# Batch 0's attention as a written-out software pipeline, its denominators on DVE, and the sign of the float64 weights moved from ACT to DVE

## The chip, the cores and the metric

The kernel runs on one core of a Trainium2 chip. The metric is the device time of one execution in microseconds; of each kernel several executions are timed and the median is given. One execution of each kernel is also profiled, and all rows below are from that one. The engines are called PE (TensorE, matrix products), DVE (VectorE), ACT (ScalarE), POOL (GpSimd) and SP (SyncE, which here only starts transfers). PE's clock has two levels, 2.4 GHz (written as a granted clock of 1.00) and 1.2 GHz (0.50).

## The reference

Three blocks follow one another on 4 sequences of 576 positions: attention with 8 heads of 64, a feed-forward block 512 to 2048 to 512 with layer norm and residual, and a mixture of 8 experts, of which each position uses one.

```python
scores = scale * np.matmul(q, k.transpose(0, 1, 3, 2))
mask_local = (rel >= 0) & (rel < stride)          # heads 0 to 3, stride 32
mask_strided = (rel >= 0) & (pos[None, :] % stride == pos[:, None] % stride)   # heads 4 to 7
scores = np.where(masks[None, :, :, :], scores, -1000000000.0)
scores = scores - np.max(scores, axis=-1, keepdims=True)
attn = np.exp(scores)
attn = attn / (np.sum(attn, axis=-1, keepdims=True) + 1e-09)
x = np.matmul(attn, v)                            # heads side by side: 512 columns
xn = (x - mu) / np.sqrt(var + 1e-06) * g_ln
x = x + np.maximum(xn @ w_ch1, 0.0) @ w_ch2
# then: an expert e per position, out = p[e] * (relu(x @ w1[e]) @ w2[e])
```

The feed-forward weights `w_ch1` and `w_ch2` arrive as float64: random float32 numbers were multiplied by a float64 factor.

## The kernel before

**Attention.** Heads are taken in pairs (`pairs`; hp 0 and 1 are local, 2 and 3 strided), and each pair is cut into three units of 3 or 4 groups (`GROUPS`). Batch 0 has four pairs, so twelve units, in the order hp 0, 2, 3, 1. A unit goes through five steps: `st_scores` (products of q with k into one PSUM tile `ps_sc`, then a maximum per row), `st_exp` (EXP on ACT), `st_norm`, `st_trans` (transposes on PE into `ps_pt`, copied to SBUF as `pt` by ACT) and `st_out` (products with v into `ps_o`, from there into `xt`, the input of the next block). `prep` transposes q and k of a pair ahead of its units; it writes them to `qbd` and `kT`.

Two ways of doing this stand side by side. In batch 0 (`FAST`) the mask is added on PE, by a product of the identity with the mask in bf16 (L300) that opens the accumulation; DVE takes the maximum (L316) and subtracts it (L317), one EXP covers the unit (L328), the denominators come from products of a constant matrix with `pt` (L372), and DVE reads them (L378), takes their RECIPROCAL over all columns (L379) and multiplies the output by it (L397). In the other batches one custom DVE instruction per group (L320) adds the mask and gives the extremum, one EXP per group (L331) also gives the sum, and `st_norm` does an addition, a RECIPROCAL on 3 or 4 columns (L341) and a scaling (L342).

Batch 0 runs alone at the start, in the loop at the end of the setup. Per turn it calls up to five steps for different units, and the scheduler of the framework then places the instructions by its own estimates, unless `keep` pins an instruction to the program's order. `st_out` adds two products of 256 columns (`keep_clock`, L285) that write to a tile nobody reads. The loads are dealt out on SP's queue by `ORD`, small ones between large ones.

**The feed-forward block.** 2304 positions are cut into 9 chunks of 256; chunk c has 16 slices f of the hidden layer, and for each `mm1` (L613, 12 products), a ReLU split in two parts (ACT L615, DVE L616) and `mm2` (L629, 12 products). The list `order` starts with chunk 0 alone, then mixes chunks 0 and 1. `ln_0`, `ln_2` and `ln_split` make chunk 0's normalized input `xc` (mean products L510 and L516, copy L523, subtraction L525, scaling L596 and L597). Attention of batches 1 to 3 is laid into this block at the places `SPANS`.

**The weights.** 32 tiles of 128x512 float64 numbers are turned into float32 by integer work, and then into a high and a low part (fp32r): `w_low` shifts the low word on DVE (L443); `w_sign` on ACT writes the sign as a half float into the low word (L449) and takes the absolute value of the high word (L450); `w_high` joins the words on DVE (L455); `w_split` casts (L469, by DVE for the first four tiles, by ACT after that) and POOL subtracts (L470). `turns` and `joins` list what is done in which turn, and `weights_next` does one turn; six turns fall in the attention of batch 0, the others in the feed-forward block while chunks 0 and 1 are worked on.

## Time and profile before

| what | us |
|---|---|
| median of 3 runs (lowest to highest) | 916.74 (914.50 to 918.66) |
| the profiled execution, its time | 914.36 |
| its span, first to last instruction | 912.5 |
| PE busy | 873.2 (96%) |
| DVE busy | 474.3 (52%) |
| ACT busy | 368.9 (40%) |
| POOL busy | 152.2 (17%) |

Busy times are unions of the instructions' times on an engine; a matrix product's record contains its latency, so PE reads as busy also where products leave room. The mean granted clock of PE is 0.962 over the span. The shares are averages over stages that differ much: the first 72 us, in which batch 0's attention runs, have to be looked at by themselves. Where a row has a bracket at its end, it is the idle time of the engine ahead of the first of these instructions and what ended it.

### The profile page before, as it was taken

The numbers are of one execution on the slowest core, as the hardware profiler recorded it, in microseconds if no ns is written. First come the engines' busy times: TensorE is split into PE (matmuls) and PEld (weight loads), VectorE is DVE, ScalarE is ACT, GpSimd is POOL, SyncE is SP. The second block draws the span as 40 slices with busy tenths as digits, with TensorE's granted clock in tenths as the row PEclk, the third lists the DMA queues.
The fourth block names the chain that finished last, engine by engine and source line by source line (L and its number), as shares of the span: only waits on it lengthen the run. The fifth ranks groups of instructions, "written<-read, shape, count | busy, mean of one in ns | idle before, by whom it ended". The sixth has DMA issues, their size and how long they took to land. (4 is left out here: it accounts for less than half of the span.)

```text
span 912.5 us, 18019 instructions
## 1 busy us (share of the span) xinstructions
PE 873.2 (96%) x6644; PEld 782.2 (86%) x6644; DVE 474.3 (52%) x1560; ACT 368.9 (40%) x919; POOL 152.2 (17%) x163
## 2 busy tenths in 40 slices
PE   7888899899999999999999999999999999999994
PEld 5657888899999999899999999999877787787773
DVE  3778756537775646657555464675722134111541
ACT  2448879943354423354231212242112244222551
POOL 2013323312020020120121212020131111110100
PEclk8757989999999999999999999999999999999999
DMA  9850444310222201210000000511374364510730
GB/s 218 219 188 1 117 108 133 91 48 1 74 52 62 57 2 27 68 43 17 28 2 24 2 24 1 185 49 47 139 265 143 139 224 157 194 48 24 285 114 15
DMA packets 95024, 82.92 MB, mean 91 GB/s; under 512 B 67395, under 2 KB 75589, under 8 KB 94920
## 3 DMA queue, kind: packets, MB, share of 16 engines
q1 hardware_dynamic: 87656, 65.41, 24.2%
q0 software_dynamic: 3632, 11.11, 3.6%
q10 hardware_dynamic: 3632, 5.09, 1.6%
q8 instruction: 55, 0.90, 0.4%
q14 instruction: 49, 0.40, 0.1%
HBM read 72.08 MB, written 10.30 MB: 90 GB/s over the span
## 5 line engine op out<-in xcount | busy, mean ns | idle before, releaser
L629 PE MATMUL acc<-h,w 128*128 128x256 f32 x1728 | 246.2, 290 | 1.0 <-DVE h L616 1.0
L613 PE MATMUL ps_h<-xc,w 128*128 128x256 f32 x1728 | 242.6, 288 | 2.5 <-ACT xc L596 1.7
L613 PEld LDWEIGHTS ps_h<-xc,w 128*128 128x128 f32 x1728 | 222.7, 195 | 5.8 <-ACT xc L596 2.4
L629 PEld LDWEIGHTS acc<-h,w 128*128 128x128 f32 x1728 | 219.9, 192 | 3.6 <-DVE h L616 1.4
L615 ACT ACTIVATE h<-ps_h 128x256 fp32r<-128x256 f32 x144 | 55.6, 386 | 220.6 <-PE ps_h L613 206.1
L616 DVE SCALAR_TENSOR_TENSOR h<-ps_h,h 128x256 fp32r<-128x256 f32 x144 | 60.7, 421 | 93.7 <-ACT h L615 93.3
L1341 PE MATMUL ps_h<-wx,xs 128*128 128x512 f32 x360 | 87.6, 398 | 0.8 <-DVEq L1268 0.8
L1369 PE MATMUL ps_y<-wx,ht 128*128 128x512 f32 x360 | 85.9, 394 | 0.0
L1341 PEld LDWEIGHTS ps_h<-wx,xs 128*128 128x128 f32 x360 | 66.6, 188 | 15.8 <-DVEq L1268 1.3
L1369 PEld LDWEIGHTS ps_y<-wx,ht 128*128 128x128 f32 x360 | 66.5, 188 | 13.3
L470 POOL TENSOR_TENSOR w<-stg,w 128x512 fp32r<-128x512 f32 x32 | 45.2, 1412 | 136.1 <-ACT w L469 69.6
L1372 ACT ACTIVATE y<-ps_y,pr 128x512 f32<-128x512 f32 x19 | 13.1, 688 | 89.2 <-PE ps_y L1369 61.6
L331 ACT ACTIVATE sm<-sm,st 108x54 f32<-108x54 f32 (+1 forms) x120 | 41.4, 348 | 15.5 <-DVE st L320 15.3
L449 ACT ACTIVATE stg<-stg 128x512 f16<-128x512 f32 x32 | 43.9, 1371 | 0.7 <-DVE stg L443 0.6
L867 DVE TENSOR_TENSOR xs<-ps_tx,xs 128x512 fp32r<-128x512 f32 x15 | 10.4, 691 | 64.0 <-ACTq L1268 45.8
L1344 ACT ACTIVATE h<-ps_h 128x512 f32<-128x512 f32 x30 | 16.3, 595 | 62.0 <-PE ps_h L1341 62.0
L759 DVE TENSOR_TENSOR wx<-raw,wx 128x1024 fp32r<-128x1024 f32 x32 | 37.5, 1220 | 1.7 <-ACT wx L756 1.3
L304 PE MATMUL ps_sc<-kT,qbd 128*128 128x96 f32 (+1 forms) x280 | 34.8, 263 | 1.6 <-DVE xt L399 0.7
L304 PEld LDWEIGHTS ps_sc<-kT,qbd 128*128 128x128 f32 (+1 forms) x280 | 32.2, 182 | 2.9 <-DVE xt L399 0.9
L756 ACT CAST wx<-raw 128x1024 fp32r<-128x1024 f32 x32 | 31.8, 1061 | 5.7 <-PE acc L629 4.1
L1373 POOL DMA_INDIRECT out_dram<-y,idx x15 | 15.1, 1005 | 113.0 <-ACT y L1372 71.3
L455 DVE SCALAR_TENSOR_TENSOR stg<-stg 128x512 int32<-128x512 int32 x32 | 25.1, 785 | 15.3 <-ACT stg L450 14.9
(375 smaller groups left out, 1203.9 us busy)
## 6 DMA issues: line engine op xcount, KB each, us to landing
stg<-in_moe_w_ch_dram SPq DMA_DIRECT2D x32, 512.0 KB
raw<-in_moe_w_dram SPq DMA_DIRECT2D x16, 1024.0 KB
raws<-in_moe_w_dram SPq DMA_DIRECT2D x16, 1024.0 KB
...
```

The lines of the kernel that those rows point to most:

```text
L304: pe.matmul(ps[0:m, i, :], qbd[:, q0:q0 + w, :].rearrange("p s j -> p (s j)"), kT[:, k0:k0 + n], start=not fast, stop=not fast or i == ng - 1)
L331: act.activation(sm[0:m, i, :], sm[0:m, i, :], AF.Exp, bias=st[0:m, 0, i:i + 1], scale=-1.0, accum_out=st[0:m, 1, i:i + 1])
L449: keep(act.activation(t.bitcast(F16)[..., 1], f32(t[..., 1]), AF.Copy, scale=2.0 ** -112))
L470: keep(pool.tensor_tensor(w[:, 1], r, f32(w[:, 0]), op=ALU.subtract))
L613: pe.matmul(ps, w[:, a, d, o:o + 128], xcs[c][:, b_, d, :], start=(i == 0), stop=(i == 11))
L615: act.activation(h[:, 0, :], ps, AF.Relu)
L616: dve.scalar_tensor_tensor(h[:, 1, :], ps, 0.0, f32(h[:, 0, :]), op0=ALU.max, op1=ALU.subtract)
L629: pe.matmul(accs[c][d // 2][:, d % 2, :], w[:, a, f % 2, d * 128:(d + 1) * 128], h[:, b_, :], start=(f == 0 and (a, b_) == (0, 0) and d % ...
L756: act.copy(wx[i][:, 0, :], raw[i // 2][:, i % 2, :])
L759: dve.tensor_tensor(wx[i][:, 1, :], raw[i // 2][:, i % 2, :], f32(wx[i][:, 0, :]), op=ALU.subtract)
L1341: pe.matmul(hp_[fg], s_[:, a, d, :], wx[d][:, b_, 512 * fg:512 * fg + 512], start=(i == 0), stop=(i == 11))
L1369: pe.matmul(ps, s_[a][:, f, :], wx[4 + f // 2][:, b_, 512 * (f % 2):512 * (f % 2) + 512], start=(i == 0), stop=(i == 23))
```

## The change

- `MODES` takes the place of `FAST` and gives each unit one of three ways. Mode 2 (batch 0, hp 0 and 2): mask by PE, DVE takes only the minimum, and ACT reads the scores from PSUM, one EXP per group with the minimum as bias. Mode 1 (batch 0, hp 3 and 1, and all of batch 1): mask by PE, minimum and subtraction on DVE, one EXP per unit. Mode 0 (batches 2 and 3) is the way that batches 1 to 3 had. So batch 1 changes from mode 0 to mode 1.
- In modes 1 and 2 DVE sums the EXPs over the keys, and `st_norm` then does what it did in mode 0. The denominator products, the wide RECIPROCAL and the final multiplication are gone; `st_out` copies, on DVE in mode 2 and on ACT in mode 1 of batch 0.
- q is scaled by -1/8 where `prep` copies it, so the scores come out negated and the maximum becomes a minimum.
- Batch 0's loop is written out: step i does the scores of unit i, the normalization of unit i-1, the transposes of i-2 and the output of i-3, and all instructions of PE, ACT and DVE in it are kept in the program's order (`Pin`). At the end of each step stand five products of 512 columns on zeros (six in the first three steps), and two after each of the first pair's two `prep` calls.
- `prep` of batch 0 takes its PSUM tiles from another pool (`ps_m`), and a fourth buffer for the EXPs is added (`SM0`).
- Loads of batch 0 come pair by pair, the first weight tile after three pairs.
- The sign of a weight: `w_low` gets a second DVE instruction that masks the sign bit of the high word and joins it to the low word; ACT's L449 goes.

```diff
...
-FAST = (0,)
+MODES = {(0, 0): 2, (0, 2): 2, (0, 3): 1, (0, 1): 1, 1: 1}
...
-NEG = -1.0e9 / SCALE
+NEG = -1.0e9
...
-SMB, SM0, PT0, TL = 2, 3, 2, 1
-WARM0, WARM, LB = 10, 2, 5
+SMB, SM0, PT0, TL = 2, 4, 2, 1
+WARM0, WARM, LB = 10, 5, 5
...
-    pe, act, dve, pool, sp = nc.tensor, nc.scalar, nc.vector, nc.gpsimd, nc.sync
+    pinned = [False]
+    class Pin:
+        def __init__(self, eng):
+            self.eng = eng
+        def __getattr__(self, name):
+            fn = getattr(self.eng, name)
+            if not pinned[0] or name == "dma_start":
+                return fn
+            return lambda *args, **kw: tc.keep_in_program_order(fn(*args, **kw))
+    pe, act, dve = Pin(nc.tensor), Pin(nc.scalar), Pin(nc.vector)
+    pool, sp = nc.gpsimd, nc.sync
...
-            ps = side_r([128, 3 * QT], "ps_tr")
+            ps = (ps_m.tile([128, 512], F32, tag="m", name="ps_tr")[:, 0:3 * QT] if b == 0 else side_r([128, 3 * QT], "ps_tr"))
...
-                act.copy(dst(qbd[0:64, 0:S, 0]), s_[0:64])
-                (act.copy if half and b else dve.tensor_copy)(dst(qbd[64:128, 0:S, 1]), s_[64:128])
+                act.activation(dst(qbd[0:64, 0:S, 0]), s_[0:64], AF.Copy, scale=-SCALE)
+                if half and b:
+                    act.activation(dst(qbd[64:128, 0:S, 1]), s_[64:128], AF.Copy, scale=-SCALE)
+                else:
+                    dve.tensor_scalar(dst(qbd[64:128, 0:S, 1]), s_[64:128], -SCALE, None, op0=ALU.mult)
...
+    def mode_of(b, hp):
+        return MODES.get((b, hp), MODES.get(b, 0))
...
-        fast = b in FAST
+        mode = mode_of(b, hp)
...
-        if fast:
+        if mode:
...
-            pe.matmul(ps[0:m, i, :], qbd[:, q0:q0 + w, :].rearrange("p s j -> p (s j)"), kT[:, k0:k0 + n], start=not fast, stop=not fast or i == ng - 1)
+            pe.matmul(ps[0:m, i, :], qbd[:, q0:q0 + w, :].rearrange("p s j -> p (s j)"), kT[:, k0:k0 + n], start=not mode, stop=not mode or i == ng - 1)
...
-        sms[b, hp, u0] = (sm, st)
-        if fast:
-            mx = st[0:m, 0, 0:ng]
-            return [lambda: dve.tensor_reduce(mx, ps[0:m], axis=AX.X, op=ALU.max),
-                    lambda: dve.tensor_tensor(sm[0:m], ps[0:m], mx.unsqueeze(2).to_broadcast([m, ng, n]), op=ALU.subtract)]
+        sms[b, hp, u0] = (sm, st, ps)
+        mn = st[0:m, 0, 0:ng]
+        if mode:
+            new = [lambda: dve.tensor_reduce(mn, ps[0:m], axis=AX.X, op=ALU.min)]
+            if mode == 1:
+                new.append(lambda: dve.tensor_tensor(sm[0:m], ps[0:m], mn.unsqueeze(2).to_broadcast([m, ng, n]), op=ALU.subtract))
+            return new
         def part(i):
-            dve.tensor_tensor_reduce(sm[0:m, i, :], ps[0:m, i, :], mask(i), -SCALE, 3.0e38, ALU.add, ALU.min, st[0:m, 0, i:i + 1])
+            dve.tensor_tensor_reduce(sm[0:m, i, :], ps[0:m, i, :], mask(i), 1.0, 3.0e38, ALU.add, ALU.min, st[0:m, 0, i:i + 1])
...
     def st_exp(b, hp, u0):
...
-        if b in FAST:
-            act.activation(sm[0:m], sm[0:m], AF.Exp, scale=SCALE)
+        mode = mode_of(b, hp)
+        if mode == 1:
+            act.activation(sm[0:m], sm[0:m], AF.Exp, scale=-1.0)
...
-            act.activation(sm[0:m, i, :], sm[0:m, i, :], AF.Exp, bias=st[0:m, 0, i:i + 1], scale=-1.0, accum_out=st[0:m, 1, i:i + 1])
+            act.activation(sm[0:m, i, :], (ps if mode else sm)[0:m, i, :], AF.Exp, bias=st[0:m, 0, i:i + 1], scale=-1.0, **({} if mode else dict(accum_out=st[0:m, 1, i:i + 1])))
     def st_norm(b, hp, u0):
...
-        if b in FAST:
-            return []
-        return [
+        todo = [
             lambda: dve.tensor_scalar(rs, rs, 1e-9, None, op0=ALU.add),
...
+        if mode_of(b, hp):
+            todo.insert(0, lambda: dve.tensor_reduce(rs, sm[0:m], axis=AX.X, op=ALU.add))
+        return todo
     def st_trans(b, hp, u0):
...
-        fast = b in FAST
-        ps = side([128, 2, ng, w] if fast else [128, 1, ng, w], "ps_o")
+        ps = side([128, ng, w], "ps_o")
...
-                pe.matmul(ps[64 * j:64 * j + 64, 0, i, 0:k], vv[0:min(n, k) if hp > 1 else n, i, j, :], pt[0:min(n, k) if hp > 1 else n, i, j:2 * k:2], start=True, stop=True)
-        if fast:
-            for j in range(2):
-                pe.matmul(ps[64 * j:64 * j + 64, 1], mean_w[0:n, 0:64], pt[0:n, :, j::2], start=True, stop=True)
-        if b == 0:
-            keep_clock(pt.rearrange("p g m -> p (g m)")[0:n, 0:256].bitcast(BF16).rearrange("p (n w) -> p n w", w=2)[:, :, 1], WARM)
-        o = ps[:, 0].rearrange("p g q -> p (g q)")
-        if fast:
-            rs = pt.rearrange("p g m -> p (g m)")[:, 0:ng * w]
-            dve.tensor_scalar(rs, ps[:, 1].rearrange("p g q -> p (g q)"), float(DM), 1e-9, op0=ALU.mult, op1=ALU.add)
-            dve.reciprocal(rs, rs)
+                pe.matmul(ps[64 * j:64 * j + 64, i, 0:k], vv[0:min(n, k) if hp > 1 else n, i, j, :], pt[0:min(n, k) if hp > 1 else n, i, j:2 * k:2], start=True, stop=True)
+        o = ps.rearrange("p g q -> p (g q)")
...
-            if fast:
-                dve.tensor_tensor(dst, cut(o), cut(rs), op=ALU.mult)
-            else:
-                (dve.tensor_copy if i % 2 else act.copy)(dst, cut(o))
+            (dve.tensor_copy if (i % 2 if b else mode_of(b, hp) > 1) else act.copy)(dst, cut(o))
...
         keep(dve.tensor_single_scalar(t[..., 0], t[..., 0], 29, op=ALU.logical_shift_right))
+        keep(dve.scalar_tensor_tensor(t[..., 0], t[..., 1], -2 ** 31, t[..., 0], op0=ALU.bitwise_and, op1=ALU.bitwise_or))
...
-        keep(act.activation(t.bitcast(F16)[..., 1], f32(t[..., 1]), AF.Copy, scale=2.0 ** -112))
         keep(act.activation(f32(t[..., 1]), f32(t[..., 1]), AF.Abs, scale=2.0 ** -112))
...
-    def weights_next():
-        for fn, i in turns[nw[0]] + joins[nw[0]]:
+    def weights_turn():
+        for fn, i in turns[nw[0]]:
...
+    joined = [0]
+    def weights_join():
+        while joined[0] < nw[0]:
+            for fn, i in joins[joined[0]]:
+                fn(i)
+            joined[0] += 1
+    def weights_next():
+        weights_turn()
+        weights_join()
...
-    load_qk(*pairs[0])
-    load_v0(0)
-    load_qk(*pairs[1])
-    big = [hold(load_w, 0), hold(load_w, 1), hold(load_qk, *pairs[2]), hold(load_w, 2), hold(load_w, 3), hold(load_qk, *pairs[3]), hold(load_w, 4), hold(load_w, 5)]
-    small = [hold(load_v0, i) for i in range(1, 4)]
-    for n in ORD:
-        load_mixed(sum((big[i] for i in n[0]), []), sum((small[i] for i in n[1]), []))
+    for i in range(4):
+        load_qk(*pairs[i])
+        load_v0(i)
+        if i > 1:
+            load_w(i - 2)
+    for i in range(2, W_START):
+        load_w(i)
...
-    while pos[0] < NSTEP or any(fifo.values()):
-        i = pos[0]
-        do_x, do_n = bool(fifo["x"]), take("n", 1)
-        do_t, do_o = bool(fifo["t"]), bool(fifo["o"])
-        if do_x:
-            do("x")
-        if i < NSTEP:
-            begin(do_n)
-        else:
-            pos[0] += 1
-            for p in [p for un in do_n for p in st_norm(*un)]:
-                p()
-            fifo["t"] += do_n
-        if do_t:
-            do("t")
-        if do_o:
-            un = fifo["o"][0]
-            do("o")
-            if un == (0, 1, 0):
-                ln_0()
-            if un == (0, 1, 3):
-                ln0 = [ln_2, ln_split]
-        if i > WI and nw[0] < W_START * (i - WI) // (NSTEP + 2 - WI):
-            weights_next()
+    pinned[0] = True
+    us = [(b, hp, u0) for b, hp in pairs[:4] for u0, _ in GROUPS[hp]]
+    for nm in "qk":
+        prep(*pairs[0], nm)
+        keep_clock(idle, 2)
+    for i in range(len(us) + 3):
+        new, old = st_scores(*us[i]) if i < len(us) else [], st_norm(*us[i - 1]) if 0 < i <= len(us) else []
+        for p in old + new:
+            p()
+        if 1 < i < len(us) + 2:
+            st_trans(*us[i - 2])
+        if i > 2:
+            st_out(*us[i - 3])
+        if i < len(us):
+            st_exp(*us[i])
+        weights_join()
+        if i < 9 and i % 3:
+            prep(*pairs[i // 3 + 1], "qk"[i % 3 - 1])
+        keep_clock(idle, WARM + (i < 3))
+        if i > 2 and us[i - 3] == (0, 1, 0):
+            ln_0()
+        if i > 2 and us[i - 3] == (0, 1, 3):
+            ln0 = [ln_2, ln_split]
+        if i > WI and nw[0] < W_START:
+            weights_turn()
...
+    weights_join()
+    pinned[0] = False
...
```

How the order moves on the engines is shown at three places. All instructions of the written-out loop have one line in the new program, L84.

DVE in the front, where the scores of units 9 and 10 meet the output of unit 6. `st` holds extremum and sum, `first` the EXPs, `stg` a weight tile. Before:

```order
L316 TENSOR_REDUCE st<-ps_sc 128x3
L378 TENSOR_SCALAR first<-ps_o 128x216
L317 TENSOR_TENSOR first<-ps_sc,st 128x288
L379 RECIPROCAL first<-first 128x216
L316 TENSOR_REDUCE st<-ps_sc 128x3
L397 TENSOR_TENSOR xt_331<-ps_o,first 128x12x8
L397 TENSOR_TENSOR xt_362<-ps_o,first 128x12x8
L397 TENSOR_TENSOR xt_387<-ps_o,first 128x12x2
```

Now (step 10, from the normalization of unit 9 to the conversion of weights behind it):

```order
L84 TENSOR_REDUCE st<-first 128x3
L84 TENSOR_SCALAR st<-st 128x3
L84 RECIPROCAL st<-st 128x3
L84 TENSOR_TENSOR first<-first,st 128x288
L84 TENSOR_REDUCE st<-ps_sc 128x3
L84 TENSOR_TENSOR first<-ps_sc,st 128x288
L84 SCALAR_TENSOR_TENSOR stg<-stg 128x512
L84 CAST w_0_600<-stg 128x4x128
L84 TENSOR_SCALAR stg<-stg 128x512
L84 SCALAR_TENSOR_TENSOR stg<-stg 128x512
```

The sum and three operations on few columns take the place of the read and the RECIPROCAL on 216 columns, and each step ends with the weights' four instructions, of which the last is the sign.

PE at the end of the front, the last units' transposes (`ps_pt`) and outputs (`ps_o`). Before:

```order
L350 MATMUL ps_pt<-iw,first 96x128 x6
L369 MATMUL ps_o<-first,v_191 64x64 x6
L372 MATMUL ps_o<-first,mean_w 64x192 x2
L285 LDWEIGHTS first
L285 MATMUL idle_ps<-first 128x256
L285 LDWEIGHTS first
L285 MATMUL idle_ps<-first 128x256
L350 MATMUL ps_pt<-iw,first 96x128 x3
```

Now:

```order
L84 MATMUL ps_pt<-iw,first 96x128 x3
L84 MATMUL ps_o<-first,v_210 64x64 x6
L84 LDWEIGHTS spare
L84 MATMUL idle_ps<-spare 128x512
L84 LDWEIGHTS spare
L84 MATMUL idle_ps<-spare 128x512
L84 LDWEIGHTS spare
L84 MATMUL idle_ps<-spare 128x512
L84 LDWEIGHTS spare
L84 MATMUL idle_ps<-spare 128x512
L84 LDWEIGHTS spare
L84 MATMUL idle_ps<-spare 128x512
```

The denominator products are gone and five products on zeros stand where two on EXPs stood.

DVE right behind the front, where the first weights are converted for `mm1` and `mm2` (L616, now L639, is the second half of `h`). Before:

```order
L443 TENSOR_SCALAR stg<-stg 128x512
L616 SCALAR_TENSOR_TENSOR h<-ps_h,h 128x256
L455 SCALAR_TENSOR_TENSOR stg<-stg 128x512
L443 TENSOR_SCALAR stg<-stg 128x512
L525 TENSOR_TENSOR xt_362<-xt_362,mu 128x512 x2
```

Now:

```order
L454 TENSOR_SCALAR stg<-stg 128x512
L639 SCALAR_TENSOR_TENSOR h<-ps_h,h 128x256
L455 SCALAR_TENSOR_TENSOR stg<-stg 128x512
L466 SCALAR_TENSOR_TENSOR stg<-stg 128x512
L454 TENSOR_SCALAR stg<-stg 128x512
L548 TENSOR_TENSOR xt_397<-xt_397,mu 128x512
```

The sign pass (L455 of the new file) stands between the shift and the join (L466), on the engine that also makes `h` and `xc`.

## Rows read from the trace of the kernel before

**Rows 1.** Stretches: length, busy us per engine (instructions), PE clock, DMA share, GB/s

```profile
14.00:31.00 17.00, 16.14 (x107) 12.56 (x108) 8.17 (x18) 5.03 (x14) 0.00 (x0) 0.50 1.06 237
32.00:41.00 9.00, 8.17 (x102) 5.96 (x102) 6.65 (x19) 4.15 (x10) 0.00 (x0) 1.00 1.00 283
41.00:72.00 31.00, 25.83 (x170) 16.40 (x168) 24.86 (x51) 13.63 (x23) 5.65 (x4) 0.50 0.47 151
72.00:79.00 7.00, 6.66 (x27) 5.96 (x28) 6.70 (x13) 5.26 (x10) 1.64 (x1) 0.52 0.01 2
116.00:123.00 7.00, 6.71 (x31) 6.71 (x32) 3.67 (x22) 3.20 (x9) 1.29 (x1) 0.52 0.01 2
72.00:101.00 29.00, 28.24 (x187) 26.97 (x188) 23.68 (x51) 24.02 (x38) 10.90 (x7) 0.82 0.02 4
```

**Rows 2.** In order of time, both ends of the front: start, us, engine, instruction

```profile
7.72 0.88 PE L304 MATMUL ps_sc<-kT,qbd 128*128 128x96 f32 x6 [0.17 <-ACT kT L274]
...
69.12 1.05 PE L516 MATMUL ps_mu<-xt,mean_w 128*128 128x256 f32 x2
...
71.90 1.94 PE L613 MATMUL ps_h<-xc,w 128*128 128x256 f32 x6 [1.73 <-ACT xc L596]
```

**Rows 3.** By source line, whole run: count, shortest/median/longest ns, first and last start

```profile
L378 DVE TENSOR_SCALAR first<-ps_o x12: 289/357/383, 20.6 to 71.8; 128x192 f32<-128x192 f32 x6, 128x216 f32<-128x216 f32 x4, 128x162 f32<-128x162 f32 x2
L379 DVE RECIPROCAL first<-first x12: 1166/1348/1504, 21.0 to 72.5; 128x192 f32<-128x192 f32 x6, 128x216 f32<-128x216 f32 x4, 128x162 f32<-128x162 f32 x2
L316 DVE TENSOR_REDUCE st<-ps_sc x12: 320/390/458, 8.6 to 55.5; 128x3 f32<-128x288 f32 x6, 108x4 f32<-108x216 f32 x4, 108x3 f32<-108x162 f32 x2
L317 DVE TENSOR_TENSOR first<-ps_sc,st x12: 262/390/457, 12.9 to 57.3; 128x288 f32<-128x288 f32 x6, 108x216 f32<-108x216 f32 x4, 108x162 f32<-108x162 f32 x2
L331 ACT ACTIVATE sm<-sm,st x120: 299/342/420, 107.6 to 431.6; 108x54 f32<-108x54 f32 x66, 128x96 f32<-128x96 f32 x54
L341 DVE RECIPROCAL st<-st x36: 165/176/178, 109.5 to 432.2; 128x3 f32<-128x3 f32 x18, 108x4 f32<-108x4 f32 x12, 108x3 f32<-108x3 f32 x6
L342 DVE TENSOR_TENSOR sm<-sm,st x36: 319/422/911, 109.7 to 432.5; 128x288 f32<-128x288 f32 x18, 108x216 f32<-108x216 f32 x12, 108x162 f32<-108x162 f32 x6
L358 ACT COPY first<-ps_pt x12: 422/475/513, 16.4 to 66.7; 96x384 f32<-96x384 f32 x6, 54x432 f32<-54x432 f32 x4, 54x324 f32<-54x324 f32 x2
L443 DVE TENSOR_SCALAR stg<-stg x32: 417/424/1551, 31.6 to 201.3; 128x512 int32<-128x512 int32 x32
L449 ACT ACTIVATE stg<-stg x32: 1340/1372/1397, 37.8 to 202.3; 128x512 f16<-128x512 f32 x32
L455 DVE SCALAR_TENSOR_TENSOR stg<-stg x32: 679/694/1799, 40.9 to 204.4; 128x512 int32<-128x512 int32 x32
```

**Rows 4.** In order of time, PE's products at full clock and (54.08) at half

```profile
9.21 0.29 PE L300 MATMUL ps_sc<-mask_loc,iw 128*128 128x288 bf16 x1
9.34 0.80 PE L304 MATMUL ps_sc<-kT,qbd 128*128 128x96 f32 x6
...
54.08 1.43 PE L304 MATMUL ps_sc<-spare 128*128 128x96 f32 x6
...
112.66 0.49 PE L350 MATMUL ps_pt<-iw,sm 128*96 128x128 f32 x3
...
123.91 0.41 PE L265 MATMUL ps_tr<-iw,qnat 96*128 96x96 f32 x3
...
128.81 0.57 PE L369 MATMUL ps_o<-pt,v 96*64 96x64 f32 x12 [0.62 <-ACT qbd L277]
```

**Rows 5.** In order of time, DVE's join beside POOL's subtraction

```profile
58.55 1.42 POOL L470 TENSOR_TENSOR w<-stg,w 128x512 fp32r<-128x512 f32 x1 [12.30 <-DVE w L469]
58.72 1.80 DVE L455 SCALAR_TENSOR_TENSOR stg<-stg 128x512 int32<-128x512 int32 x1
```

**Rows 6.** PE's waits at 100 to 125 and 125 to 170: us, times, longest

```profile
PE ps_var L549 <- ACT pt L358: 1.2, 1, 1.2
...
PE ps_o L369 <- ACT pt L358: 1.3, 1, 1.3
```

More of the change, by code (lines that the diff above doesn't have):

```diff
@@ L93, in attention_moe_moe @@
     pool.memset(mask_loc, 0.0)
-    pool.affine_select(out=mask_loc, in_=mask_loc, pattern=[[-2, 128]], compare_op=ALU.is_ge, fill=NEG, base=2 * STR, channel_multiplier=1)
-    pool.affine_select(out=mask_loc, in_=mask_loc, pattern=[[2, 128]], compare_op=ALU.is_ge, fill=NEG, base=-1, channel_multiplier=-1)
+    pool.affine_select(out=mask_loc, in_=mask_loc, pattern=[[-2, 128]], compare_op=ALU.is_ge, fill=-NEG, base=2 * STR, channel_multiplier=1)
+    pool.affine_select(out=mask_loc, in_=mask_loc, pattern=[[2, 128]], compare_op=ALU.is_ge, fill=-NEG, base=-1, channel_multiplier=-1)
     mask_str = cst.tile([128, 3, NA], F32, name="mask_str")
     pool.memset(mask_str, 0.0)
-    pool.affine_select(out=mask_str, in_=mask_str, pattern=[[-2 * NA, 3], [-2, NA]], compare_op=ALU.is_ge, fill=NEG, base=0, channel_multiplier=1)
-    pool.affine_select(out=mask_str, in_=mask_str, pattern=[[2 * NA, 3], [0, NA]], compare_op=ALU.is_ge, fill=NEG, base=2 * NA - 1, channel_multiplier=-1)
+    pool.affine_select(out=mask_str, in_=mask_str, pattern=[[-2 * NA, 3], [-2, NA]], compare_op=ALU.is_ge, fill=-NEG, base=0, channel_multiplier=1)
+    pool.affine_select(out=mask_str, in_=mask_str, pattern=[[2 * NA, 3], [0, NA]], compare_op=ALU.is_ge, fill=-NEG, base=2 * NA - 1, channel_multiplier=-1)
     mask_str = mask_str.rearrange("p a b -> p (a b)")
@@ L343, in st_norm @@
         ]
+        if mode_of(b, hp):
+            todo.insert(0, lambda: dve.tensor_reduce(rs, sm[0:m], axis=AX.X, op=ALU.add))
+        return todo
     def st_trans(b, hp, u0):
-        sm, st = sms.pop((b, hp, u0))
+        sm, st, ps = sms.pop((b, hp, u0))
         ng, w, n, m = shape_of(hp, u0)
```

4 lines of the change are left out of this document (2 added, 2 removed).

## The prediction

> **What bounds the kernel now.** I read the table by stretches first, then the chain of instructions in order of time around two marks, then the durations by source line, last the waits. The kernel is a front (batch 0's attention, alone on the chip) and a long body of expert products. In the body TensorE (PE) is the bound: it is busy 28.24 of 29 us at 72 to 101 [rows 1]. The front has no single bound. Its marks are the first score product, at 7.72, and the first product of the feed-forward layer (L613), at 71.90 [rows 2]: 64.2 us for twelve units. What the reader is to see there is the clock. PE's granted clock is 0.50, that is 1.2 GHz, at 14 to 31 and at 41 to 72, and full (2.4 GHz) only at 32 to 41 [rows 1]. In the slow stretches PE is busy 16.14 of 17 and 25.83 of 31 us, DVE 24.86 of those 31. The same six records of score products take 0.80 us at full clock and 1.43 at half [rows 4]. So the front is a chain between a PE at half speed and a DVE that carries one RECIPROCAL over 192 or 216 columns per unit (1.35 us, twelve of them, 16.2 us in all [rows 3]).
>
> **The change part by part: the front.** Removed per unit on DVE: the denominators' read (L378, 0.36) and the wide RECIPROCAL (L379, 1.35), and on PE the two denominator products with their share of padding. Added per unit on DVE: a sum over keys, then three row operations. The trace has no reduction that reads SBUF; the nearest row, the maximum over the same shape, is 0.32 to 0.46, median 0.39 (L316), and I take that. With the small addition and RECIPROCAL at 0.17 each (L341) and the scaling at 0.42 (L342) it is 1.15 [rows 3]. DVE is 1.71 - 1.15 = 0.56 lighter per unit, 6.7 us in all; six units also lose the subtraction (L317, 0.39), 2.3 more. Against it stand the sign passes of the six weight tiles begun here, at 0.69 like L455, the same form: 4.1. DVE nets about 5 us, so DVE's sum alone is no large gain; the steps have to be followed.
>
> The loop now has fifteen steps. PE per step at full clock: mask 0.13 (9.21 to 9.34), scores 0.80, transposes 0.49, outputs 0.57 [rows 4], and five products of 512 columns on zeros, 5 x 512 / 2.4 GHz = 1.07: together 3.06. Six steps also carry the q or k transposes, 2 x 0.41 [rows 4]. The first seven steps have four of those, so PE needs 3.5 each, and 0.1 more for the sixth zero product of the first three. DVE's own loop there is minimum 0.39, three EXPs on ScalarE (ACT) at 0.34, then 1.15: 2.6 [rows 3], with copies beside it. I take 3.7 per step: PE's sum and little waiting. Steps 7 to 11 also convert weights. DVE then has 1.15 + 0.39 + 0.39 and, of the weights, the join 0.69, a cast that I take like L443 (0.42), the shift 0.42 and the new sign 0.69 [rows 3]: 4.15. A pass of this form that starts just after POOL's subtraction took 1.80 instead of 0.69 [rows 5]; one such wait per step gives 5.25. I take 5.1, near that row. The rest (last normalization 1.15, transposes 0.49, the copy 0.47 (L358), outputs 0.57 [rows 3, 4], and the 2.8 from the last mean product to L613 [rows 2]) is 5.5. From a first score at 8.0 (four zero products now stand before it): 8.0 + 7 x 3.7 + 5 x 5.1 + 5.5 = 64.9. I add 2 for a fall of the clock in the late steps, where PE works only 3.1 to 3.9 of 5.1 us: L613 at 67, **5 us earlier**. Bounds: 3.1, 4.15 and 5 give 55.5 (16 us gained); 4.6, 6.0 and 8 give 78 (6 lost). The loads in another order I cost at nothing: batch 0's q, k and v are only moved ahead of weights that the shift first reads at step 6, some 33 us in.
>
> In this trace the clock went to half at 41 straight from a stretch in which PE was busy 8.17 of 9 us, and stayed there with PE busy five sixths of the time [rows 1]. The Trainium skill, "TensorE: Matmul & The Clock Gate", section "What's actually happening", says that the half rate is the state after an idle window and that activity releases it. By that rule the 2 us for a fall would be 0; the trace disagrees, since no idle window stands ahead of that fall.
>
> **Behind the front.** (1) At 72 to 79 PE is busy 6.66 us at clock 0.52 [rows 1]. If the zero products hand over a full clock, half of that, 3.3, is the most that comes back; part of it waits for xc, so I take -2 (0 to -3.3). (2) Batch 1 gets its masks by PE: fourteen products at 0.13 on the bounding engine, 1.8, with weight loads +2 (1.8 to 4). (3) ACT loses L449, 32 x 1.37 = 44 us, and in batch 1 two or three EXPs per unit. PE's waits on ACT's copy of the transposed weights are 1.2 and 1.3 [rows 6], and right behind the first of these the clock is 0.52 at 116 to 123, with 6.71 us busy, so 3.3 lost [rows 1]: at most -5.8 in these places.  I take -3.5 (0 to -8, since smaller waits lie further on). (4) DVE gets the sign. It is busy 23.68 of 29 us at 72 to 101, where seven tiles pass [rows 1]: 7 x 0.69 = 4.8 makes 28.5, just full; what ACT no longer delays hides most of it. Queued behind each pass on DVE are the second half of h and xc, for which PE waits. I take +1.5 (0 to +7, at 1.80 per pass). If the cover goes (no waits on ACT left to fill), the 4.8 are paid.
>
> The 0.69 and 1.80 of one form are a row of this trace [rows 5]. The Trainium skill, "SBUF — State Buffer", section "SBUF: two separate sides", says that a DVE operation with two SBUF inputs and a GpSimd operation that reads SBUF exclude one another for the whole instruction, whoever comes first. The trace agrees. By that rule alone, every pass would pay the full wait and term (4) would be +7.
>
> **Sum:** -5 - 2 + 2 - 3.5 + 1.5 = **-7**. The profiled execution took 914.36 us, of which 912.5 are its span; 914.36 - 7 = 907.4. The median of the runs, 916.74 (914.5 to 918.66), lies 2.4 above that execution, so for a median I expect 907.4 + 2.4 = 909.8, rounded down to **909**, since my late steps lean to the slow bound.
>
> **Rivals.** *Full clock, free DVE* (0.20): the zero products hold 2.4 GHz through the whole front and POOL rarely meets the sign passes. Then steps take 3.5 and 4.5, L613 comes at 8 + 24.5 + 22.5 + 5.5 = 60.5, 11.4 early, and ACT's relief is 5: -11.4 - 2 + 2 - 5 + 0 = -16.4, about 900. For it: padding is now 2560 columns per step in place of two times 256. It is also what comes out by the rule on the clock that the Trainium skill's page above states. Against it: the late steps' DVE sum.
> *Given back* (0.20): the front gains 5 to 7, but DVE, full at 72 to 101, paces the first weights at 1.80 per sign, +7: about 916. For it: 23.68 of 29 us. Against it: much of PE's work there can be taken from chunk 1.
> *Half clock in the fixed order* (0.14), the slower side: the order is now rigid and zero products stand ahead of the next scores. If the clock falls at the early handovers, as it did at 14, PE's step is 3.4 x 1.43 / 0.80 = 6.1 against 3.7, and PE holds it there, all fifteen steps: 8 + 15 x 5.5 (mean with the lighter last ones) = 90, 18 us later; -1 behind it: about 933. It decides from some five early steps at half: 5 x 2.4 = 12 eats all the gains. For it: half clock in 48 of 64 us before. Against it: no long gaps of PE are left by the order.
> The rest (0.46) is my forecast, 909, with its own range 903 to 915. That the change doesn't do what it says I leave without a chance: the program's order shows the fixed order and the new passes.
>
> **Chances and range.** About 0.5% of the time, 4.6 us, can be told from no change. Faster (below 912.2): 0.39 of the forecast's 0.46 and the first rival's 0.20, 0.59. Within: 0.07 and most of the second rival, 0.17, so 0.24. Slower: 0.14 and 0.03, so 0.17. The range 898 to 922 leaves out half of the clock rival's far end above, the lowest part of the first rival below, and the worst of the DVE bound.
>
> **What would show it.** The granted clock at 14 to 31 and 41 to 72; the start of the first product of that layer, 67 (60 to 62 for the first rival, about 90 for the third); the mean of the sign pass (0.69 to 1.3); the stretch after it, where DVE's busy share should rise and PE's waits on ACT's copy vanish. Wrong would be a front that ends at 72 or later, or an early L613 with a body that ends as late as before.

## The result and the profile after

The changed kernel takes 904.0 us (median of four runs, 903.27 to 905.7) where the kernel before takes 916.9 (by now four runs, 914.5 to 918.66): a ratio of 0.986, 95% interval 0.984 to 0.989, so 10 to 15 us faster. The forecast was 909 in a range of 898 to 922. The profiled execution took 905.7 us (span 903.9) against 914.36, 8.7 less. The medians are 12.9 apart because the profiled execution of before lies 2.6 below its median and that of after 1.7 above its own.

The same stretches as in [rows 1], now of the changed kernel (length; busy us and instructions of PE, PEld, DVE, ACT, POOL; granted clock; DMA share; GB/s):

```profile
14.00:31.00 17.00, 15.43 (x139) 10.54 (x140) 10.31 (x37) 7.38 (x26) 0.00 (x0) 0.90 0.98 254
32.00:41.00 9.00, 8.14 (x98) 6.18 (x97) 8.24 (x27) 4.32 (x11) 0.92 (x1) 1.00 1.00 270
41.00:72.00 31.00, 26.80 (x197) 18.93 (x192) 26.80 (x51) 13.22 (x38) 7.64 (x6) 0.83 0.31 89
72.00:79.00 7.00, 5.67 (x44) 5.20 (x43) 7.00 (x13) 4.90 (x10) 2.37 (x2) 1.00 0.23 46
116.00:123.00 7.00, 5.18 (x61) 4.74 (x60) 6.50 (x17) 3.17 (x7) 1.58 (x2) 1.00 0.51 136
72.00:101.00 29.00, 24.15 (x198) 23.33 (x197) 28.09 (x55) 14.75 (x30) 11.12 (x7) 1.00 0.52 166
```

Two things differ. The clock, 0.50 at 14 to 31 and at 41 to 72 before, is 0.90 and 0.83. And at 72 to 101 the full engine is DVE, 28.09 of 29 us against 23.68, while PE fell from 28.24 to 24.15 and ACT from 24.02 to 14.75.

PE's marks in order of time (start, us, instruction, in brackets the idle time ahead and what ended it); they answer to [rows 2]:

```profile
7.88 0.83 PE L84 MATMUL ps_sc<-kT,qbd 128*128 128x96 f32 x6
...
31.64 0.88 PE L84 MATMUL ps_sc<-kT,qbd 128*108 128x54 f32 x8
...
45.39 0.80 PE L84 MATMUL ps_sc<-spare 128*128 128x96 f32 x6
48.42 0.50 PE L84 MATMUL ps_pt<-iw,first 128*96 128x128 f32 x3 [2.23 <-DVE first L84]
48.86 0.54 PE L84 MATMUL ps_o<-first,v 54*64 54x54 f32 x12
49.33 2.32 PE L84 MATMUL idle_ps<-spare 128*128 128x512 bf16 x5
53.56 0.88 PE L84 MATMUL ps_pt<-iw,first 128*96 128x128 f32 x3 [1.91 <-DVE first L84]
...
64.11 2.10 PE L636 MATMUL ps_h<-xc,w 128*128 128x256 f32 x13
```

The first product of the feed-forward layer, L613 before and L636 now, starts at 64.11 instead of 71.90. The scores of the twelfth unit start at 45.39, and from there PE waits for DVE. What DVE does in one of those late steps (DVE and POOL in order of time):

```profile
44.54 0.43 DVE L84 CAST w<-stg 128x512 fp32r<-128x512 f32 x1
44.88 0.42 DVE L84 TENSOR_SCALAR stg<-stg 128x512 int32<-128x512 int32 x1
45.05 1.42 POOL L481 TENSOR_TENSOR w<-stg,w 128x512 fp32r<-128x512 f32 x1 [3.56 <-DVE w L84]
...
45.34 1.67 DVE L84 SCALAR_TENSOR_TENSOR stg<-stg 128x512 int32<-128x512 int32 x1
...
46.93 0.44 DVE L84 TENSOR_REDUCE st<-first 128x3 f32<-128x288 f32 x1
47.41 0.17 DVE L84 TENSOR_SCALAR st<-st 128x3 f32<-128x3 f32 x1
47.61 0.17 DVE L84 RECIPROCAL st<-st 128x3 f32<-128x3 f32 x1
47.82 0.46 DVE L84 TENSOR_TENSOR first<-first,st 128x288 f32<-128x288 f32 x1
48.20 0.45 DVE L84 TENSOR_REDUCE st<-ps_sc 128x3 f32<-128x288 f32 x1
...
52.16 0.44 DVE L84 TENSOR_REDUCE st<-first 128x3 f32<-128x288 f32 x1
...
53.42 0.45 DVE L84 TENSOR_REDUCE st<-ps_sc 128x3 f32<-128x288 f32 x1
```

One step is 46.93 to 52.16, 5.2 us. The sign pass is the row at 45.34: 1.67 us, begun 0.29 after a subtraction on POOL and ended half a us behind it. The minimum at 53.42 belongs to the scores of 45.39: DVE is eight us behind PE. (A TENSOR_REDUCE of `ps_sc` is a unit's minimum, one of `first` its sum over keys.)

Behind the front, the leading waits of PE at 64 to 101, then at 100 to 125 (us, times, longest):

```profile
PE ps_sc L320 <- DVE kT L288: 2.8, 1, 2.8
...
PE ps_h L636 <- DVE xc L620: 1.2, 1, 1.2
PE acc L652 <- DVE h L639: 0.9, 2, 0.7
```

```profile
PE ps_pt L374 <- DVE sm L363: 1.8, 1, 1.8
...
PE ps_o L392 <- DVE kT L288: 1.0, 1, 1.0
```

The waits on ACT's copy in [rows 6] have no counterpart here or at 125 to 170; what PE waits for now is mostly DVE.

### The profile page after: what moved, and what is told of

The parts are those of the page before. It is cut to its first block, busy times and chain, and to the rows that moved or that the text cites. A ratio compares the mean times of both kernels' runs of the same rounds, so it can differ in the third digit from the quotient of the medians.

```text
span 903.9 us, 17997 instructions
## 1 busy us (share of the span) xinstructions
PE 865.7 (96%) x6668; PEld 773.4 (86%) x6668; DVE 502.0 (56%) x1552; ACT 326.3 (36%) x847; POOL 153.5 (17%) x163
## 5 line engine op out<-in xcount | busy, mean ns | idle before, releaser
L636 PE MATMUL ps_h<-xc,w 128*128 128x256 f32 x1728 | 237.8, 286 | 1.2 <-DVE xc L620 1.2
L636 PEld LDWEIGHTS ps_h<-xc,w 128*128 128x128 f32 x1728 | 219.3, 192 | 3.0 <-DVE xc L620 1.3
L639 DVE SCALAR_TENSOR_TENSOR h<-ps_h,h 128x256 fp32r<-128x256 f32 x144 | 60.5, 420 | 89.6 <-ACT h L638 89.0
L890 DVE TENSOR_TENSOR xs<-ps_tx,xs 128x512 fp32r<-128x512 f32 x15 | 10.4, 691 | 63.8 <-ACTq L1294 45.2
L1384 DVE TENSOR_TENSOR ht<-ps_th,ht 128x512 fp32r<-128x512 f32 x30 | 19.3, 685 | 24.5 <-ACT ht L1383 24.2
L354 ACT ACTIVATE sm<-sm,st 108x54 f32<-108x54 f32 (+1 forms) x80 | 27.6, 348 | 13.2 <-DVE st L342 13.1
L892 DVE SCALAR_TENSOR_TENSOR pr<-io_e,e_rep,xg 128x8 f32<-128x8 f32 x15 | 3.4, 229 | 51.0 <-ACT y L1398 45.8
L324 PE MATMUL ps_sc<-kT,qbd 128*108 128x54 f32 (+1 forms) x240 | 29.4, 261 | 0.0
L324 PEld LDWEIGHTS ps_sc<-kT,qbd 128*108 128x108 f32 (+1 forms) x240 | 27.6, 182 | 0.6 <-issue 0.4
```

The costliest lines, as they stand in the source:

```text
L324: pe.matmul(ps[0:m, i, :], qbd[:, q0:q0 + w, :].rearrange("p s j -> p (s j)"), kT[:, k0:k0 + n], start=not mode, stop=not mode or i == ng - 1)
L354: act.activation(sm[0:m, i, :], (ps if mode else sm)[0:m, i, :], AF.Exp, bias=st[0:m, 0, i:i + 1], scale=-1.0, **({} if mode else dict(acc ...
L636: pe.matmul(ps, w[:, a, d, o:o + 128], xcs[c][:, b_, d, :], start=(i == 0), stop=(i == 11))
L639: dve.scalar_tensor_tensor(h[:, 1, :], ps, 0.0, f32(h[:, 0, :]), op0=ALU.max, op1=ALU.subtract)
L1384: dve.tensor_tensor(s_[1][:, 4 * g:4 * g + 4, :], ps, f32(s_[0][:, 4 * g:4 * g + 4, :]), op=ALU.subtract)
```

## The experiments

The theory after this comparison: DVE, not the clock, sets the end of the front, and the sign on DVE is paid there and earned back behind it, where ACT was late. A letter (theory A, B and so on) holds for the run whose expectation names it. The rivals: the zeros and the clock are the gain; the relief of ACT is the gain; the order of loads matters. The table has the first product of the layer (us), the lead over the kernel before (us, from the starts in the two traces; at the layer's first product, 192 and 576 products later and at its last, counting the products of `mm1` and `mm2` together), and the ratio of times to the kernel before with its interval.

| kernel | first product | lead at 0 | 192 | 576 | last | ratio |
|---|---|---|---|---|---|---|
| changed | 64.11 | 7.8 | 10.4 | 9.3 | 10.8 | 0.986 (0.984 to 0.989) |
| changed, second time | 63.00 | 8.9 | 8.9 | 11.1 | 12.3 | 0.987 (0.985 to 0.990) |
| changed, sign on ACT | 59.09 | 12.8 | 19.2 | 9.0 | 9.7 | 0.987 (0.984 to 0.991) |
| changed, no zeros | 66.52 | 5.4 | 8.0 | 6.8 | 8.4 | 0.988 (0.985 to 0.992) |
| changed, batch 1 as before | 62.99 | 8.9 | 11.8 | 6.4 | 7.1 | 0.990 (0.987 to 0.994) |
| changed, denominators as before | 70.54 | 1.4 | 1.9 | 3.7 | 5.3 | 0.993 (0.991 to 0.996) |
| changed, cast behind the sign | 62.51 | 9.4 | 12.5 | 9.7 | 10.7 | 0.987 (0.985 to 0.990) |
| changed, loads as before | 62.32 | 9.6 | 12.3 | 11.1 | 12.7 | 0.988 (0.985 to 0.991) |
| sign of 6 tiles on ACT | 59.05 | 12.9 | 13.5 | 15.3 | 15.7 | 0.983 (0.979 to 0.986) |
| sign of 14 tiles on ACT | 57.30 | 14.6 | 21.0 | 16.1 | 16.9 | 0.982 (0.979 to 0.985) |
| the same, three zeros | 60.79 | 11.1 | 16.5 | 11.6 | 12.6 | 0.982 (0.979 to 0.984) |
| before, sign on DVE | 75.16 | -3.3 | -0.7 | -6.0 | -6.5 | 1.007 (1.004 to 1.010) |
| before, padding times five | 85.73 | -13.8 | -13.8 | -13.8 | -13.8 | 1.016 (1.012 to 1.021) |

The second line gives the scale: one program, two executions, and the marks differ by one to two us. A lead is read with that much doubt. All leads are against one execution of the kernel before, 2.6 us faster than its median.

**Sign back on ACT.**

```diff
-        keep(dve.scalar_tensor_tensor(t[..., 0], t[..., 1], -2 ** 31, t[..., 0], op0=ALU.bitwise_and, op1=ALU.bitwise_or))
+        keep(act.activation(t.bitcast(F16)[..., 1], f32(t[..., 1]), AF.Copy, scale=2.0 ** -112))
```

> The changed kernel with the sign back on ACT (two ACT passes of 1.37 us per tile, no sign pass on DVE). Theory A, DVE paces the late front: in the changed kernel four sign passes of 1.66 to 1.67 us stand in DVE's chain at 40 to 57 us, in steps of 5.2; without them these steps are some 3.9, the first product of the feed-forward layer comes at 59 to 60 instead of 64.1, ACT fills up behind it (14.75 of 29 us at 72 to 101, plus nine passes of 1.37, is 27) and PE's waits on ACT come back for 2 to 3 us: about 901 against 904. Theory B, relief of ACT is what the body gained by: the first product comes at 60 to 64, but the gain behind it is lost and 3.5 to 6 us more: 907 to 910.

The first product came at 59.09 as theory A has it, but the time is that of the changed kernel: 905.8 (before on that chip: 918.4). So neither theory alone. In the late front DVE's step is now 4.15 us, 42.12 to 46.27:

```profile
41.45 0.43 DVE L84 CAST w<-stg 128x512 fp32r<-128x512 f32 x1
41.79 0.43 DVE L84 TENSOR_SCALAR stg<-stg 128x512 int32<-128x512 int32 x1
42.12 0.45 DVE L84 TENSOR_REDUCE st<-first 128x3 f32<-128x288 f32 x1
42.60 0.79 DVE L84 TENSOR_SCALAR st<-st 128x3 f32<-128x3 f32 x1
...
46.27 0.45 DVE L84 TENSOR_REDUCE st<-first 128x3 f32<-128x288 f32 x1
```

Behind it the stretches of the same kernel:

```profile
72.00:101.00 29.00, 23.86 (x192) 22.61 (x192) 22.69 (x55) 24.49 (x37) 11.69 (x8) 1.00 0.50 162
125.00:170.00 45.00, 40.92 (x337) 38.55 (x338) 25.36 (x67) 33.00 (x59) 13.11 (x10) 0.85 0.40 101
```

DVE has room at 72 to 101 (22.69 of 29), and the lead grows to 19.2. Then 10 of it go between the 192nd and 576th product. ACT is busy 33.00 of 45 us at 125 to 170, the clock is 0.85 there, where the changed kernel has 1.00, and PE's waits at 101 to 205 are on ACT again, as in [rows 6]:

```profile
PE ps_o L392 <- ACT pt L382: 1.7, 2, 1.0
...
PE ps_tr L279 <- ACT qbd L292: 1.2, 2, 0.9
PE ps_tr L279 <- ACT pt L382: 1.2, 1, 1.2
```

In the new order the sign on DVE costs 4 to 5 us in the front; from the first product to the last it is worth 6 (lead 7.8 to 10.8, against 12.8 to 9.7). The two cancel.

**The zeros left out.**

```diff
-        keep_clock(idle, 2)
...
-        keep_clock(idle, WARM + (i < 3))
```

> The changed kernel without the products on zeros in and ahead of the fixed order (the ten at the very start stay). Theory A, the zeros hold the clock: PE has some 2.1 us of work in a step of 3.2, the granted clock goes to 0.50 in large parts of 14 to 64 us as in the kernel before, the first product of the layer comes at 70 or later and the layer starts at half clock: 911 to 916. Theory C, the fixed order and the lighter DVE carry the gain and the zeros are ballast: steps get shorter by up to 1.1 us where PE is the bound, the first product comes at 56 to 62 and the time is 898 to 903.

907.4, ratio 0.988: neither. The clock did what A says (stretches of this kernel):

```profile
14.00:31.00 17.00, 13.28 (x96) 10.99 (x95) 10.24 (x33) 7.92 (x27) 0.00 (x0) 0.60 1.08 263
41.00:57.00 16.00, 11.29 (x86) 9.31 (x84) 15.28 (x36) 6.12 (x20) 4.21 (x3) 0.50 0.56 167
66.00:72.00 6.00, 6.00 (x47) 5.79 (x47) 5.97 (x10) 5.15 (x10) 1.80 (x2) 1.00 0.00 0
```

But the first product is only 2.4 to 3.5 us later: at 41 to 57 DVE is full, 15.28 of 16 us, and PE, though at half clock, is not (11.29). And the layer starts at full clock without zeros in the front. The zeros, with the clock that goes with them and less the time that they take themselves, are worth some 3 us at the first product, not the gain; in the time this can't be told from nothing (0.988 with 0.985 to 0.992, against 0.986 and 0.987).

**Denominators as before, in the new order.**

```diff
+        if b == 0:      # in st_norm
+            return []
...
+            for j in range(2):
+                pe.matmul(ps2[64 * j:64 * j + 64, 1], mean_w[0:n, 0:64], pt[0:n, :, j::2], start=True, stop=True)
...
+            dve.tensor_scalar(rs, ps2[:, 1].rearrange("p g q -> p (g q)"), float(DM), 1e-9, op0=ALU.mult, op1=ALU.add)
+            dve.reciprocal(rs, rs)
...
+                dve.tensor_tensor(dst, cut(o), cut(rs), op=ALU.mult)
```

> The changed kernel with batch 0's denominators made as before (two products of a constant matrix per unit, DVE's read, the wide RECIPROCAL and the final multiplication; no sum over keys); order, zeros and modes stay. DVE per unit: 0.36 + 1.35 + the multiplication in place of the copy, against 1.15. Theory D, the order carries the gain: the denominators come off the path between scores and transposes, DVE's late steps of 5.2 us grow by some 0.6 and a first product at 64 to 67 follows: 904 to 907. Theory F, the lighter denominators carry it: the twelve RECIPROCALs, 16 us, come back into a DVE that is the bound from unit 7 on, and the first product comes at 69 or later: 909 to 914.

First product at 70.54 and 911.8, as theory F has it. Half of the gain is gone, though the clock at 41 to 72 is 0.84, no lower than in the changed kernel. DVE's late step of this kernel, 49.27 to 55.60, is 6.3 us, 1.1 longer than in the changed kernel:

```profile
49.27 0.44 DVE L84 TENSOR_REDUCE st<-ps_sc 128x3 f32<-128x288 f32 x1
49.75 0.46 DVE L84 TENSOR_TENSOR first<-ps_sc,st 128x288 f32<-128x288 f32 x1
50.12 0.37 DVE L84 TENSOR_SCALAR first<-ps_o 128x216 f32<-128x216 f32 x1
50.53 1.50 DVE L84 RECIPROCAL first<-first 128x216 f32<-128x216 f32 x1
52.07 0.53 DVE L84 TENSOR_TENSOR xt<-ps_o,first 128x96 f32<-128x96 f32 x3
...
55.60 0.44 DVE L84 TENSOR_REDUCE st<-ps_sc 128x3 f32<-128x288 f32 x1
```

The row at 52.07 is the final multiplication, which in these late units takes the place of a copy on ACT; it is part of what this run undoes. Of the parts undone this is the largest, 6.4 to 7.5 us at the first product, and the only one whose interval lies clear of the changed kernel's.

**Padding alone, in the old order.**

```diff
-WARM0, WARM, LB = 10, 2, 5
+WARM0, WARM, LB = 10, 10, 5
```

> The kernel before with one thing changed: ten padding products of 256 columns behind each unit's output instead of two, 2560 columns as in the new kernel, in the old order. Theory A, padding holds the clock in either order: granted clock near 1.00 at 14 to 66 and the first product of the layer at 64 to 68 instead of 71.9: 908 to 913. Theory D, the order does it: PE in the old order waits for DVE between units whatever is padded, the clock stays at 0.50 in most of 14 to 72, the padding at half clock (2.1 us per unit) lies in PE's way, and the first product comes at 72 to 85: 917 to 930.

930.5, theory D, just past the upper ends of its ranges (930, and 85 for the first product). The clock stayed at 0.50 at 14 to 31 with PE busy 16.16 of 17 us, and the first product came at 85.73:

```profile
14.00:31.00 17.00, 16.16 (x108) 12.01 (x109) 5.47 (x13) 3.40 (x9) 0.00 (x0) 0.50 1.05 208
```

**Sign on DVE alone, in the kernel before.**

```diff
+        keep(dve.scalar_tensor_tensor(t[..., 0], t[..., 1], -2 ** 31, t[..., 0], op0=ALU.bitwise_and, op1=ALU.bitwise_or))
...
-        keep(act.activation(t.bitcast(F16)[..., 1], f32(t[..., 1]), AF.Copy, scale=2.0 ** -112))
```

> The kernel before with one part of the change alone: the sign joined by DVE, ACT's pass away. Theory A: six more passes of 0.69 to 1.8 us on a DVE that is busy 24.86 of 31 us at 41 to 72 move the first product of the layer from 71.9 to 74 to 79; behind it ACT's relief gives 1 to 3 back: 916 to 921, same or slower. Theory B: relief of ACT is worth more than DVE's passes cost: 909 to 913.

923.8 (before on that chip: 918.4), slower by 0.4 to 1.0%. In the front it is theory A: the first product moved from 71.90 to 75.16. But the 1 to 3 us that A gives back behind the front did not stay: the lag of 3.3 is 0.7 at the 192nd product, 6.0 at the 576th and 6.5 at the last, and the time lies above A's 921. A part of this stands in the clock, 0.89 at 175 to 205, where the kernel before has 1.00; the rest is not explained. So the move of the sign is no gain by itself in either order, and what it earns behind the front in the new order, it does not earn in the old one.

**Batch 1 as before.**

```diff
-MODES = {(0, 0): 2, (0, 2): 2, (0, 3): 1, (0, 1): 1, 1: 1}
+MODES = {(0, 0): 2, (0, 2): 2, (0, 3): 1, (0, 1): 1}
```

> The changed kernel with batch 1 in mode 0, as before the change (mask by DVE's custom instruction, one EXP per group). Theory A: the fourteen mask products (2 us of PE) and the lighter ACT and DVE cancel: the first product stays at 64.1 and the time is 902 to 906. Theory B, batch 1's way is where the 3 to 4 us behind the front come from: 907 to 909, with the gain missing between the first and the 48th product of the layer. If only the mask products counted, 902.

908.5, ratio 0.990: the time of theory B, some 3 us of 917 more than the changed kernel, but the intervals overlap. The place was not the one expected: the lead is whole at 192 products (11.8) and 5.4 shorter at 576. In that part the clock of this kernel falls:

```profile
150.00:175.00 25.00, 22.21 (x184) 20.13 (x181) 18.31 (x57) 13.57 (x43) 6.28 (x4) 0.86 0.31 82
```

The changed kernel has 1.00 in the same stretch. So batch 1's new way looks like a gain and not like the cost of 2 us that I entered, but with one profile of it and overlapping intervals neither its size nor its path is settled.

**The cast behind the sign.** In each turn the shift and the sign of one tile are put ahead of the cast of another, so that POOL's subtraction no longer starts beside the sign.

```diff
-        for fn, i in turns[nw[0]]:
+        for fn, i in sorted(turns[nw[0]], key=lambda e: 2 * (e[0] is load_w) + (e[0] is w_split)):
```

> The changed kernel with each turn's shift and sign ahead of its cast instead of behind it, so that POOL's subtraction, which the cast releases, no longer runs beside the sign pass. Theory A, the sign's 1.66 us in the late front are 0.69 of work and the rest a wait for POOL: the passes at 44 to 58 fall to 0.7, one of the small operations behind the cast rises to some 0.8 as with the sign on ACT, DVE's late steps shrink from 5.2 to 4.7, and the first product comes at 61 to 63: 901 to 903 against 904. Theory H, 1.66 is what the pass costs behind a shift of the same tile: it stays, and so does the time, 904.

The sign fell to 0.69, but the wait went to another instruction behind it (DVE, then POOL, of this kernel):

```profile
44.93 0.69 DVE L84 SCALAR_TENSOR_TENSOR stg<-stg 128x512 int32<-128x512 int32 x1
45.54 0.42 DVE L84 CAST w<-stg 128x512 fp32r<-128x512 f32 x1
45.88 0.45 DVE L84 TENSOR_REDUCE st<-first 128x3 f32<-128x288 f32 x1
46.36 1.00 DVE L84 TENSOR_SCALAR st<-st 128x3 f32<-128x3 f32 x1
...
50.84 0.45 DVE L84 TENSOR_REDUCE st<-first 128x3 f32<-128x288 f32 x1
```

```profile
46.04 1.29 POOL L481 TENSOR_TENSOR w<-stg,w 128x512 fp32r<-128x512 f32 x1 [3.54 <-DMA v<-in_v_dram]
```

An addition on three columns takes 1.00 us instead of 0.17 and ends with POOL's subtraction (46.04 + 1.29 = 47.33). In all four late steps of this kernel that addition ends within 0.03 us of POOL's subtraction. That settles where the 1.66 us come from (theory A, not H). But the step shrank from 5.2 only to 5.0, not to A's 4.7, and the time is not A's 901 to 903 but that of the changed kernel run beside it, 905.6 against 905.4:

> The changed kernel itself, for a time on the same chip as the three that follow. Every theory: a ratio near 0.986 to the kernel before, first product of the layer at 64.

**Loads as before**, by putting the old block of loads into the changed kernel:

```diff
-    for i in range(4):
-        load_qk(*pairs[i])
...
+    for n in ORD:
+        load_mixed(sum((big[i] for i in n[0]), []), sum((small[i] for i in n[1]), []))
```

> The changed kernel with the old order of the loads. DVE's, ACT's and POOL's order is word for word that of the changed kernel. Theory A, the reordering is free, as costed: first product at 64, same time. Theory I, the fixed order needs it: in the kernel before, the third and fourth pairs' transposes ran at 27.7 and 39.3, in the changed kernel they run at 23.4 and 33.3; with loads that suit the old times PE, DVE and ACT stand still for 3 to 6 us, and the first product comes at 67 to 70: 907 to 911.

904.7 against 905.4 beside it: the order of the loads is free, theory A.

**Sign divided between the engines.** Both theories above point to one version: ACT for the tiles that fall into the front, DVE for the later ones.

```diff
+        if i < 6:       # 14 in the second version
             keep(act.activation(t.bitcast(F16)[..., 1], f32(t[..., 1]), AF.Copy, scale=2.0 ** -112))
...
+        if i >= 6:
             keep(dve.scalar_tensor_tensor(t[..., 0], t[..., 1], -2 ** 31, t[..., 0], op0=ALU.bitwise_and, op1=ALU.bitwise_or))
```

> The changed kernel with the sign of the first six weight tiles (those that fall into the front) on ACT and of the other 26 on DVE. With the sign on ACT for all tiles the first product came at 59.1 instead of 64.1, and the lead over the changed kernel was gone by the 576th product of the layer, lost where ACT had both passes of the later tiles. Theory A: the front's 5 us stay when the later tiles are on DVE: first product at 59 to 60, 898 to 901 against 904. Theory G: the lead is lost anyway, because the weights' pace and not the front sets when the later products can start: 903 to 906.

> The same with the first fourteen tiles on ACT and the other 18 on DVE: ACT, half idle at 64 to 101, also takes the passes of that stretch, where DVE is busy 28.09 of 29 us at 72 to 101. Theory A: first product at 59 to 60 and a lead of 17 to 19 us over the kernel before at the 192nd product (it was 19.2 with all signs on ACT), of which 3 to 7 us beyond the changed kernel's 10 to 12 stay to the end: 897 to 901. Theory G: as above, 903 to 906.

902.7 and 901.7 (before on that chip: 917.8): both times lie between the ranges of A and G. The marks are nearer to A's: first products at 59.05 and 57.30 (A had 59 to 60 for both), and the lead stays, 15.7 and 16.9 at the last product where all signs on ACT kept 9.7. With fourteen the lead at the 192nd product is 21.0 (A had 17 to 19). Both intervals overlap a little with the changed kernel's (0.984 to 0.989). The stretches of the version with fourteen:

```profile
72.00:101.00 29.00, 25.95 (x196) 25.17 (x195) 23.38 (x55) 20.75 (x33) 12.31 (x8) 0.91 0.51 162
125.00:170.00 45.00, 41.23 (x390) 38.06 (x387) 40.73 (x87) 24.32 (x56) 17.72 (x14) 1.00 0.41 109
```

DVE and ACT share the load at 72 to 101, and at 125 to 170 the clock is 1.00. With three zeros instead of five on top of that:

```diff
-WARM0, WARM, LB = 10, 5, 5
+WARM0, WARM, LB = 10, 3, 5
```

> The first fourteen tiles' sign on ACT, and three products on zeros per step instead of five. Steps 0 to 10 are some 3.2 us, of which the five zeros take 1.25 in the records. Theory A, the clock stays at 1.00 with three: steps shorten by up to 0.43 us where PE is the bound, and the first product comes 1 to 4 us before the 57.3 of the kernel with fourteen tiles on ACT: a ratio of 0.978 to 0.981 to the kernel before (that kernel had 0.982). Theory C', the clock falls to 0.50 in parts of 14 to 50 as without zeros: first product at 58 to 62, a ratio of 0.983 to 0.987.

900.7, ratio 0.982 (0.979 to 0.984), against 905.4 and 0.987 (0.985 to 0.990) of the changed kernel on the same chip: about 0.5% faster than it, and none of its six runs (898.2 to 902.7) is as slow as the fastest of the changed kernel's (903.8 to 907.9). Its clock was 0.64 at 14 to 31 and its first product 3.5 us behind the version with five, as C' has it; the ratio lies between the two theories' ranges and is that of the version with five, so three and five zeros can't be told apart.

## Why the prediction was right, and where it was not

**The sign and the size.** Faster was right; 904 instead of 909. Between profiled executions I forecast -7, and it was -8.7 (-8.6 in the spans). That this is close is partly luck: the front gave 7.8 where I had 5, the layer behind it 3.0 where I had 2, and behind the layer's last product the changed kernel then takes 2.2 longer (289.7 us to the end of the span against 287.5), for which I had no term and no run here shows a reason. The rest is the step from there to a median: I carried a distance of +2.4 over from before, and after's profiled execution lies 1.7 on the other side. That distance is no property of a kernel.

**The front** (67 forecast, 64.1 and 63.0 measured). The total is close because errors cancel. Steps 0 to 6 took 3.4 each, not 3.7 (7.88 to 31.64). Steps 7 to 10 took 3.4 too, not 5.1 (31.64 to 45.39): the step that failed is letting DVE's time set PE's steps there. DVE did take 5.2 per step, as I summed, but PE ran ahead of it, and the lag was paid at the end: 45.39 to 64.11 is 18.7 us against my 5.1 + 5.5 + 2 = 12.6. The prices themselves held: a sum over keys 0.41 (I took 0.39), one wait for POOL per step (1.67 against my 1.80), so the sign's share of a late step was right; the run with the sign on ACT gives 4 to 5 us for it in all.

**The cause.** I put the clock first and DVE's lighter sums second ("nets about 5 us, so DVE's sum alone is no large gain"). The runs turn that round: without zeros the front is 2.4 to 3.5 us longer, with the old denominators 6.4 to 7.5 (of this, about 0.5 per late step is the multiplication on DVE in place of ACT's copy). Netting the sign's passes against the sums hid that both lie on the path. The slower rival, half clock through the fixed order, did not occur; the run nearest to it, without zeros and at 0.50 to 0.60 for 14 to 57, ends its front at 66.5, far from that rival's 90.

After the change the clock falls at 49 (the five zeros at 49.33 take 2.32 us, those of the step before it 1.25), right behind PE's wait of 2.23 us. The Trainium skill, "TensorE: Matmul & The Clock Gate", section "What's actually happening", has the half rate as the state after an idle window, and activity as what ends it. That row is in line with it. The fall at 41 in the kernel before is hardly so, since PE's longest wait in the nine us ahead of it is 0.59 us; nor is the padded kernel before, which stayed at 0.50 with PE busy 16.16 of 17 us.

**Behind the front.** From the first product to the last the lead grew by 3.0 (second execution 3.4); I had -2 + 2 - 3.5 + 1.5 = -2. Term (1): the lead grew from 7.8 to 11.6 at the 24th product and stands at 10.0 at the 48th, so by 2 to 4, no less than my 2. But "if the zero products hand over a full clock" is not the reason, since the kernel without zeros gains as much there (5.4 to 9.8, then 8.0) and starts the layer at 1.00. What makes the clock full there I can't say. Term (2): batch 1 at +2 has the wrong sign by the run that undid it (some -3, intervals overlapping). Terms (3) and (4) together, -2, were -6 for the sign alone (lead 7.8 to 10.8 with it on DVE, 12.8 to 9.7 on ACT; the version with six tiles on ACT, which starts the layer at the same time as that one, goes from 12.9 to 15.7). Taken together these sizes come to more than the 3.0 that was measured: what one part is worth when it is undone alone depends on the others, as the sign shows, which earns 6 here and nothing in the old order. DVE "just full" at 28.5 of 29 was measured as 28.09, and the sign passes behind the front took 0.90 in the mean, inside my 0.69 to 1.3.

**Left open.** Whether the written-out order by itself gains anything: no run has the old loop with the new denominators; nor was mode 2 taken apart from mode 1 in batch 0. The 2.2 us lost behind the layer are open too. That the loads cost nothing was right.
